# Bucketed attention with a gated product: 305 unread TensorE products put into the first batch's instruction order, and the score banks made fixed tiles

## The chip, the cores and the metric

One NeuronCore of one Trainium2 chip runs the whole program. The metric is device time in microseconds (us), the median of three runs. Inside the core, TensorE multiplies matrices (in the profile PE; its weight loads PEld), VectorE (DVE), ScalarE (ACT) and GpSimd (POOL) do elementwise work, and SyncE (SP) issues DMAs. The engines run on their own and wait for each other by semaphores; each engine executes its instructions in the order in which the program lists them. TensorE writes only to PSUM, which DVE and ACT read.

## The reference

Attention over 4 batches, 8 heads, 768 positions, 64 features; a key counts for a query only if both fall in the same of 64 buckets (signs of 6 projections). Its output, 3072 tokens by 512, then goes through a gated product.

```
q_bits = (einsum('bhsd,dk->bhsk', q, proj) > 0); k_bits likewise; bucket = sum of bits * 2**n
scores = where(q_bucket == k_bucket, q @ k.T / sqrt(64), -1e9)
attn = exp(scores - max); attn = attn / (sum(attn) + 1e-9); x = attn @ v   -> 3072 x 512
out = ((x @ w_a) * (x @ w_b)) @ w_out        (w_a, w_b: 512 x 1536; w_out: 1536 x 512)
```

## The kernel before

**Work.** Keys and queries are split into two half-precision parts and turned so that the features lie on partitions (`split`, with `kt`, `qt` the parts, `trk`, `trq` the turned copies, `hp` a ring of buffers for the second part with the bucket bits). The masking penalty is part of the same product as the scores. For each 128 queries of a head, `qtile` (L1194) makes one score tile `s` of 128 x 768 by four matmuls (L1207); DVE takes its maximum `mx` (L1227); DVE or POOL makes `sc` and `bias` (L1235, L1239); ACT takes the exponential `e` (L1248); `e` is turned, by TensorE through PSUM tiles `et` in the first eight tiles and by DMA later (`at`), and multiplied with `v` into `av` (L1261, L1276). A finished chunk goes into `xT` and through the gated product (`moe`: `ab` L1434 and L1442, `g` L1471, `o` L1507). In the first batch the weights are loaded in 36 DMAs (L926) through three staging places, rebuilt by ACT (L937, L947), POOL (L939) and DVE (L955) into `wz`, and bounded by TensorE products `gram_w`, `gram_wo` (L973) that DVE reduces to `wst`, `wost` (L661).

**PSUM.** A partition has eight banks of 512 fp32 columns. Tag `s` has two buffers of [128, 2, 512], two banks each; tag `ab` three of one bank, `av` one. A score tile uses columns 0 to 383 of each of the two banks of its buffer (`HALF` is 384). The turned keys and queries go through `s` buffers too: twelve 128x128 half-precision blocks fill columns 0 to 511 of the first bank and 0 to 255 of the second. Other small products take only the first bank, or an `ab` buffer.

**Order.** The kernel is first written down as a list of 3727 operations with costs (`Plan.op`), numbered as they are defined (`o.seq`). `Plan.issue` (L400) then plays them through by the keys in `PLACES` and by the free buffers, and calls each operation's function at L465; the order of these calls is the order on each engine. A buffer of `Buf` is given out when the first operation that uses it is played and comes free with the last. Semaphores between engines are put in by the framework: an instruction waits for earlier instructions of other engines that read or wrote what it touches.

Of the kernel before, what the change touches and what calls it, by code (L numbers as in the profile page):

```python
# [12 lines left out]
F32 = mybir.dt.float32  # L13
# [8 lines left out]
P = 128  # L22
# [3 lines left out]
HALF = S // 2  # L26
# [5 lines left out]
CH = 256  # L32
# [222 lines left out]
)  # L255
ENGINES = {
    17: "DVE", 20: "ACT", 27: "ACT", 33: "DVE", 36: "DVE", 43: "ACT", 49: "DVE", 52: "DVE", 53: "ACT DVE",
    59: "DVE", 69: "POOL", 81: "ACT", 84: "ACT", 85: "POOL", 91: "ACT", 106: "ACT", 108: "ACT", 117: "POOL",
# [82 lines left out]
class Buf:  # L341


    def __init__(self, plan, pool, tag, bufs, shape, dtype, name, share=None, ring=None):
        self.ring = ring
        self.plan, self.pool, self.tag, self.bufs = plan, pool, tag, bufs
        self.limits = [((pool, tag), bufs)]
        if share:
            self.limits.append(((pool, tag, share[0]), share[1]))
        self.shape, self.dtype, self.name = shape, dtype, name  # L350
        self.real, self.left, self.free_at = None, 0, 0.0
# [15 lines left out]
class Plan:  # L367
# [3 lines left out]

    def __init__(self):
        self.ops, self.writer, self.readers = [], {}, {}

    def op(self, eng, dur, fn, key, r=(), w=(), svc=0.0, hold=(), sbuf=False):
        o = Op()
        o.eng, o.dur, o.fn, o.key, o.svc, o.sbuf = eng, dur, fn, key, svc, sbuf
        o.seq = len(self.ops)
        preds = set()
        for x in r:  # L380
            if x in self.writer:
                preds.add(self.writer[x])
            self.readers.setdefault(x, []).append(o.seq)
        for x in w:
            if x in self.writer:
                preds.add(self.writer[x])
            preds.update(self.readers.pop(x, ()))
            self.writer[x] = o.seq
        preds.discard(o.seq)
        o.preds = preds  # L390
        o.bufs = []
        for x in (*r, *w, *hold):
            x = x[0] if isinstance(x, tuple) else x
            if isinstance(x, Buf) and x not in o.bufs:
                o.bufs.append(x)
                x.left += 1
        self.ops.append(o)
        return o

    def issue(self):  # L400
        ops = self.ops
        for o, place in zip(ops, PLACES):
            o.key = place
            o.eng = ENGINES.get(o.seq, o.eng)
        for o in ops:
            o.succs, o.npred, o.ready = [], len(o.preds), 0.0
        for o in ops:
            for p in o.preds:
                ops[p].succs.append(o)
        free = {e: 0.0 for e in ("PE", "ACT", "DVE", "POOL", "SP")}  # L410
        ready = {e: [] for e in free}
        for o in ops:
            if not o.npred:
                for e in o.eng.split():
                    ready[e].append(o)
        live = {}
        dma_free = 0.0
        held = set()
        port = 0.0
        done = 0  # L420
        now = 0.0
        events = [0.0]
        releases = []

        def can(o):
            need = {}
            for b in o.bufs:
                if b not in held:
                    for k, _ in b.limits:
                        need[k] = need.get(k, 0) + 1  # L430
            return all(live.get(k, 0) + need.get(k, 0) <= n for b in o.bufs for k, n in b.limits)

        while done < len(ops):
            now = heapq.heappop(events)
            while events and events[0] <= now:
                heapq.heappop(events)
            while releases and releases[0][0] <= now:
                _, k = heapq.heappop(releases)[0:2]
                for x in self.tags[k]:
                    live[x] -= 1  # L440
            for e in free:
                if free[e] > now:
                    continue
                if e == "POOL" and port > now:
                    continue
                best = None
                shut = e == "DVE" and free["POOL"] > now + PORT_WAIT
                for o in ready[e]:
                    if shut and o.sbuf:
                        continue  # L450
                    if o.ready <= now and (best is None or (o.key, o.seq) < (best.key, best.seq)) and can(o):
                        best = o
                if best is None:
                    continue
                o = best
                for x in o.eng.split():
                    ready[x].remove(o)
                for b in o.bufs:
                    if b not in held:
                        held.add(b)  # L460
                        for k, _ in b.limits:
                            live[k] = live.get(k, 0) + 1
                dur = o.dur
                if isinstance(dur, dict):
                    o.fn(e)  # L465
                    dur = dur[e]
                else:
                    o.fn()
                end = now + dur
                if e == "DVE" and o.sbuf:  # L470
                    end = max(now, free["POOL"]) + dur
                    port = end
                free[e] = end
                if o.svc:
                    dma_free = max(dma_free, end) + o.svc
                    fin = dma_free + DMA_TAIL
                else:
                    fin = end + (PE_TAIL if e == "PE" else 0.0)
                for b in o.bufs:
                    b.left -= 1  # L480
                    b.free_at = max(b.free_at, fin + HOP)
                    if not b.left:
                        if b.ring is not None:
                            b.ring.append(b.real)
                        if not hasattr(self, "tags"):
                            self.tags = []
                        self.tags.append([k for k, _ in b.limits])
                        heapq.heappush(releases, (b.free_at, len(self.tags) - 1))
                        heapq.heappush(events, b.free_at)
                for s in o.succs:  # L490
                    s.ready = max(s.ready, end if s.eng == e and not o.svc else fin + HOP)
                    s.npred -= 1
                    if not s.npred:
                        for x in s.eng.split():
                            ready[x].append(s)
                        heapq.heappush(events, max(now, s.ready))
                heapq.heappush(events, end)
                done += 1
            if not events and done < len(ops):
                raise RuntimeError("no operation can start")  # L500
        return now
# [3 lines left out]
def attention_moe(ctx: ExitStack, tc: tile.TileContext, q, k, v, proj, w_a, w_b, w_out, cst, out):  # L505
    nc = tc.nc
# [3 lines left out]
    pp = ctx.enter_context(tc.tile_pool(name="pp", bufs=1, space=PSUM))  # L510

    plan = Plan()
    op = plan.op

    def buf(tag, shape, dtype, name, bufs=2, pool=None, share=None):
        return Buf(plan, pool or p2, tag, bufs, shape, dtype, name, share)

    def f3(name, share):


        return buf("f3", [P, S], F32, name, NF3, share=share)

    def two(name, share):


        return buf("two", [P, 2 * S], F16, name, NTWO, share=share)

    def psum(name, tag="s"):

        return buf(tag, [P, 2, CH if tag == "ab" else 512], F32, name, {"s": 2, "ab": 3}[tag], pp)  # L530

    def f32(ap):
        return ap.bitcast(F32)
# [51 lines left out]
    onesr = cp.tile([P, P], BF16, tag="onesr", name="onesr")  # L585
# [79 lines left out]
    def gram(x, cols, key, toks, stat, stok, tag, name):  # L665


        ps = psum(f"gram_{name}", tag)

        def products():  # L670
            high = x().bitcast(BF16).rearrange("p (n two) -> p n two", two=2)[:, :, 1]
            for i in range(cols // P):
                c = high[:, i * P : (i + 1) * P]
                nc.tensor.matmul(ps.t[:, 0, :P], lhsT=c, rhs=c, start=i == 0, stop=i == cols // P - 1)

        op("PE", 0.11 * cols / P, products, key, r=toks, w=[ps])
        op("DVE", 0.3, lambda: most_of(ps, stat), key, r=[ps], w=[stok])
# [861 lines left out]
    for b in range(NB):  # L1539
        chunks = [m for m in range(NCHUNK) if CHUNKS[m][0] == b]  # L1540
        sus = [(m, half) for m in chunks for half in range(CHUNKS[m][2])]
        for i, (m, half) in enumerate(sus):
            start, nt = done, CHUNKS[m][2]
            h0, nh = heads(m, half)
            tag = "ab" if start < 2 * UT else "s"
# [65 lines left out]
```

## Time and profile before

| what | us |
|---|---|
| median of 3 runs (902.34 to 904.34) | 903.89 |
| the profiled execution | 904.85 |
| its span, first to last instruction | 903.1 |
| outside the span | 1.75 |
| TensorE busy, share of the span | 874.0, 97% |
| VectorE busy | 625.5, 69% |
| ScalarE busy | 572.5, 63% |
| mean granted TensorE clock | 0.986 |

A busy share of 97% is an average over a first stage, in which all engines prepare keys, queries and weights, and a long second one. The clock is given as a share of full speed; its two levels are 1.2 GHz (0.5) and 2.4 GHz (1.0).

### The profile page before, as it was taken

The numbers are of one execution on the slowest core, as the hardware profiler recorded it, in microseconds if no ns is written. First come the engines' busy times: TensorE is split into PE (matmuls) and PEld (weight loads), VectorE is DVE, ScalarE is ACT, GpSimd is POOL, SyncE is SP. The second block draws the span as 40 slices with busy tenths as digits, with TensorE's granted clock in tenths as the row PEclk, the third lists the DMA queues.
The fourth block names the chain that finished last, engine by engine and source line by source line (L and its number), as shares of the span: only waits on it lengthen the run. The fifth ranks groups of instructions, "written<-read, shape, count | busy, mean of one in ns | idle before, by whom it ended". The sixth has DMA issues, their size and how long they took to land.

```text
span 903.1 us, 24309 instructions
## 1 busy us (share of the span) xinstructions
PE 874.0 (97%) x9761; PEld 676.1 (75%) x9761; DVE 625.5 (69%) x1446; ACT 572.5 (63%) x1124; POOL 451.5 (50%) x377
## 2 busy tenths in 40 slices
PE   5798999999999999999999999999999999999998
PEld 4587787777877777777777777777777777777775
DVE  6899878897778666677776686777778676633211
ACT  5985656777767777666666665667676566654222
POOL 1255456455736665644445556545556457544111
PEclk9798999999999999999999999999999999999999
DMA  8997766589998999997986798799996757754100
GB/s 309 282 328 192 129 124 147 133 187 209 183 232 155 160 157 171 181 215 157 181 169 124 142 188 163 123 205 165 184 187 140 129 133 133 147 95 96 35 24 24
DMA packets 430433, 145.31 MB, mean 161 GB/s; under 512 B 404080, under 2 KB 422640, under 8 KB 430320
## 3 DMA queue, kind: packets, MB, share of 16 engines
q1 hardware_dynamic: 430320, 143.77, 77.4%
q8 instruction: 76, 1.25, 0.6%
q14 instruction: 37, 0.30, 0.1%
HBM read 37.82 MB, written 6.29 MB: 49 GB/s over the span
## 4 chain that ended last, share of the span: by engine, by line
PE 84%; DVE 7%; DMA 3%; issue 3%; ACT 2%; POOL 1%; SPq 0%; DVEq 0%; POOLq 0%; ACTq 0%
PE ab L1442 36%; PE o L1507 19%; PE s L1207 13%; PE av L1276 10%; PE ab L1434 4%; DMA wz<-in_moe_w_out_dram 1%; DVE mx L1227 1%; DVE wz L955 1%; DMA rq<-in_q_dram 1%; DVE wz L898 1%; DMA v<-in_v_dram 1%; DMA at<-a 1%; PE qb L780 0%; PE av L1261 0%; ACT wz L937 0%
## 5 line engine op out<-in xcount | busy, mean ns | idle before, releaser
L641 POOL TENSOR_TENSOR a<-e,a 128x768 f16<-128x768 f32 x184 | 310.5, 1692 | 202.1 <-DVE a L638 87.5
L1442 PE MATMUL ab<-xT,wz 128*128 128x256 f16 (+1 forms) x3456 | 377.5, 264 | 1.5 <-DVE g L1471 1.1
L1442 PEld LDWEIGHTS <-wz 128*128 128x128 f16 x3456 | 310.9, 98 | 52.4 <-issue 3.6
L1248 ACT ACTIVATE e<-s,bias,sc 128x768 f32<-128x768 f32 x192 | 189.6, 988 | 109.5 <-DVE bias L1239 87.5
L1227 DVE TENSOR_REDUCE mx<-s 128x1 f32<-128x768 f32 x192 | 182.6, 953 | 64.9 <-PE s L1207 59.8
L1507 PE MATMUL o<-wz,g 128*128 128x512 f16 (+1 forms) x840 | 215.7, 392 | 0.1
L1487 POOL TENSOR_TENSOR g<-g,g 128x256 f16<-128x256 f32 x132 | 96.4, 730 | 169.5 <-ACT g L1482 157.0
L1207 PE MATMUL s<-trk,trq 76*128 76x384 f16 (+1 forms) x768 | 158.3, 331 | 3.3 <-ACT e L1248 2.4
L1471 DVE SCALAR_TENSOR_TENSOR g<-ab,ab,a 128x256 f32<-128x256 f32 x132 | 63.3, 479 | 106.5 <-ACT a L1463 89.2
L1276 PEld LDWEIGHTS <-at 128*128 128x128 f16 x3312 | 116.9, 98 | 16.8 <-DMA at<-a 1.8
L1507 PEld LDWEIGHTS <-g 128*128 128x128 f16 x792 | 73.9, 98 | 68.8
L1276 PE MATMUL av<-vh,at 128*128 128x64 f16 x2208 | 121.6, 193 | 1.4 <-DMA at<-a 1.4
L1463 ACT ACTIVATE a<-ab,ab 128x256 f32<-128x256 f32 x132 | 62.1, 471 | 95.2 <-PE ab L1442 79.3
L1207 PEld LDWEIGHTS <-trq 76*128 76x128 f16 (+1 forms) x768 | 70.7, 99 | 45.0 <-issue 8.8
L638 ACT CAST a<-e 128x768 f16<-128x768 f32 x105 | 87.0, 829 | 3.9 <-DMA at<-a 1.9
L1482 ACT CAST g<-g 128x256 f16<-128x256 f32 x132 | 53.0, 401 | 51.2 <-DVE g L1471 40.9
L1276 PE MATMUL av<-vl,at 128*128 128x64 f16 x1104 | 62.4, 193 | 0.0
L638 DVE CAST a<-e 128x768 f16<-128x768 f32 x71 | 42.2, 596 | 14.0 <-ACT e L1248 13.2
L1434 PE MATMUL ab<-xT,wz 128*128 128x128 f32 x384 | 48.0, 278 | 3.0 <-DVE wst L661 2.2
L1434 PEld LDWEIGHTS ab<-xT,wz 128*128 128x128 f32 x384 | 45.6, 192 | 5.4 <-DVE wst L661 2.4
L1239 DVE TENSOR_SCALAR bias<-mx,sc 128x1 f32<-128x1 f32 x180 | 38.5, 214 | 6.3
L1235 DVE TENSOR_SCALAR sc<-mx,cq 128x1 f32<-128x1 f32 x180 | 38.1, 212 | 4.8
(169 smaller groups left out, 778.5 us busy)
## 6 DMA issues: line engine op xcount, KB each, us to landing
rk<-in_k_dram SPq DMA_DIRECT2D x16, 384.0 KB, 4.1
rq<-in_q_dram SPq DMA_DIRECT2D x24, 256.0 KB, 3.4
wz<-in_moe_w_a_dram SPq DMA_DIRECT2D x12, 512.0 KB, 5.1
wz<-in_moe_w_b_dram SPq DMA_DIRECT2D x12, 512.0 KB, 5.4
wz<-in_moe_w_out_dram SPq DMA_DIRECT2D x12, 512.0 KB, 4.7
out_dram<-osb SPq DMA_DIRECT2D x24, 256.0 KB, 2.5
vr<-in_v_dram SPq DMA_DIRECT2D x12, 384.0 KB, 4.6
at<-a SPq DMA_TRANSPOSE x184, 3.5
```

The source lines that it names most:

```text
L638: {"ACT": nc.scalar.copy, "DVE": nc.vector.tensor_copy, "POOL": nc.gpsimd.tensor_copy}[e](out=out, in_=x)
L641: (nc.gpsimd if e == "POOL" else nc.vector).tensor_tensor(out=out, in0=x, in1=y, op=ALU.subtract)
L1207: nc.tensor.matmul(ps.t[:, jj, :HALF], lhsT=trq.t[rows, i, (2 * j + h) * nt + t], rhs=tr.t[rows, i, k0 : k0 + NT // 2].rearrange("p n s -> ...
L1227: lambda: nc.vector.tensor_reduce(out=mx.t[:, col], in_=halves(ps.t), axis=AX.XY, op=ALU.max, negate=True),
L1248: lambda: nc.scalar.activation(flat2(e.t), halves(ps.t), AF.Exp, bias=bias.t[:, col], scale=sc.t[:, col], accum_out=sm.t[:, u : u + 1],),
L1276: nc.tensor.matmul(av.t[:, u, :], lhsT=at.t[:, a + kt, :], rhs=w.t[:, h, kt, :], start=i == 0, stop=i == 3 * NT - 1,)
L1434: nc.tensor.matmul(pl.t[:, m, to], lhsT=wt32(m, cc, f), rhs=xt.t[:, cc * nt // NC, cc * nt % NC : cc * nt % NC + nt, :], start=cc == 0, st ...
L1442: nc.tensor.matmul(pl.t[:, m, to], lhsT=wt(m, wi, cc, f), rhs=xt.t[:, cc * nt // NC, xi, cc * nt % NC : cc * nt % NC + nt, :], start=i == ...
L1463: lambda a=a, pl=pl, gr=gr, sc_of=sc_of: nc.scalar.activation(a.t, pl.t[:, 0, :CH], AF.Copy, scale=sc_of(gr)),
L1471: lambda a=a, g32=g32, pl=pl, gr=gr, sc_of=sc_of: nc.vector.scalar_tensor_tensor(out=g32.t, in0=pl.t[:, 1, :CH], scalar=sc_of(gr + 1), in1 ...
L1487: lambda g=g, g32=g32, g_of=g_of: nc.gpsimd.tensor_tensor(out=g_of(g[1]), in0=g32.t, in1=g_of(g[0]), op=ALU.subtract),
L1507: nc.tensor.matmul(po[u].t.rearrange("p a b -> p (a b)"), lhsT=x()[:, us], rhs=w, start=f == 0 and i == 0, stop=f == NF - 1 and i == len(t ...
```

## The change

A product of the 128x128 tile of ones `onesr` with itself, written to a place that nobody reads, is issued in the numbers of `FILLS` just before the operation with that number. The place is columns 384 to 511 of the second bank of the first `s` buffer. The two `s` buffers are no longer given out by the pool: they are fixed tiles, handed round by the ring that `Buf` already has.

```diff
+FILLS = {
+    7: 30, 13: 4, 77: 3, 15: 1, 79: 2, 29: 3, 99: 12, 86: 15, 47: 9, 196: 12, 42: 11, 51: 11, 67: 11, 119: 4, 58: 6,
+    308: 16, 74: 10, 152: 19, 181: 6, 320: 9, 171: 6, 132: 6, 159: 5, 218: 8, 545: 13, 170: 4, 269: 12, 402: 16,
+    386: 5, 420: 28, 592: 8,
+}
...
         self.ops, self.writer, self.readers = [], {}, {}
+        self.fill = None
...
                 dur = o.dur
+                if o.seq in FILLS:
+                    self.fill(FILLS[o.seq])
                 if isinstance(dur, dict):
                     o.fn(e)
...
+    banks = [pp.tile([P, 2, 512], F32, tag=f"s{i}", name=f"s{i}") for i in range(2)]
+    idle_at = banks[0][:, 1, HALF:]
+
+    def fill(n):
+
+        for _ in range(n):
+            nc.tensor.matmul(idle_at, lhsT=onesr, rhs=onesr, start=True, stop=True)
+
+    plan.fill = fill
...
-        return buf(tag, [P, 2, CH if tag == "ab" else 512], F32, name, {"s": 2, "ab": 3}[tag], pp)
+        if tag == "s":
+            return Buf(plan, pp, tag, 2, [P, 2, 512], F32, name, None, banks)
+        return buf(tag, [P, 2, CH], F32, name, 3, pp)
```

The keys stand in the order in which the plan plays them. The list below says, for the groups from the twelfth on, which operation follows, when it started before, and which reader of the second bank of the first `s` buffer the plan plays last ahead of the group. Ahead of the first eleven groups (102 products) that reader had ended in the trace before TensorE came to the group.

| key | products | operation that follows, and its start before | last reader ahead of it |
|---|---|---|---|
| 51 | 11 | `kt` transposes, 25.38 | DVE `mx` at 24.55 |
| 67, 119, 58 | 11, 4, 6 | `kt` 29.98, `et` 31.11, `kt` 32.46 | ACT `e` at 28.86 (67, 119), ACT `trk` at 30.99 (58) |
| 308, 74, 152 | 16, 10, 19 | `ps_w` 36.98, `kt` 37.93, score 40.28 | DVE `trk` at 36.84 |
| 181 | 6 | score 42.44 | ACT `trk` at 40.13 |
| 320, 171, 132 | 9, 6, 6 | `gram_wo` 44.59, score 46.90, `av` 48.81 | DVE `mx` at 43.97 |
| 159 | 5 | `et` 50.25 | ACT `e` at 49.43 |
| 218 | 8 | score 59.53, in the other `s` buffer | DVE `mx` at 59.59 |
| 545, 170 | 13, 4 | `gram_q` 67.03, `av` 67.97 | ACT `e` at 65.90 |
| 269 | 12 | score 72.94, in the other `s` buffer | DVE `mx` at 73.58 |
| 402 | 16 | first `ab` 77.56 | DVE `mx` at 73.58 |
| 386, 420 | 5, 28 | `gram_w` 83.48, `ab` 90.58 | ACT `e` at 77.77 |
| 592 | 8 | score 113.49 | ACT `e` at 105.24 |

## Rows read from the trace of the kernel before

**Rows 1.** Busy time by stretch: stretch, length, PE, PEld, DVE, ACT, POOL, clock, DMA.
```profile
0.00:90.58 90.58, 69.70 (x692) 60.05 (x692) 77.56 (x163) 65.10 (x92) 33.01 (x37) 0.87 0.87 277
90.58:226.00 135.42, 132.74 (x1628) 105.93 (x1629) 112.62 (x243) 90.61 (x168) 72.02 (x57) 1.00 0.78 155
226.00:500.00 274.00, 273.59 (x3204) 209.60 (x3203) 195.98 (x489) 192.80 (x397) 151.77 (x123) 1.00 0.92 174
```

**Rows 2.** Waits of DVE, 0 to 90.58: total us, times, longest.
```profile
DVE wz L955 <- ACT wz L937: 1.5, 1, 1.5
DVE mx L1227 <- PE s L1207: 1.1, 2, 0.8
DVE mx L1227 <- PE ps_k L612: 1.1, 1, 1.1
...
DVE po_t_k L624 <- PE ps_k L612: 0.7, 1, 0.7
DVE wst L661 <- PE gram_w L973: 0.5, 2, 0.3
...
DVE vst L661 <- PE gram_v L674: 0.3, 1, 0.3
```

**Rows 3.** Busy time by stretch around the low clock, columns as in rows 1.
```profile
21.00:29.00 8.00, 6.37 (x51) 5.36 (x52) 6.42 (x16) 8.00 (x10) 3.29 (x4) 0.57 0.80 268
38.00:50.00 12.00, 9.82 (x67) 7.38 (x67) 9.43 (x14) 10.57 (x16) 4.95 (x8) 0.57 0.93 253
69.00:77.00 8.00, 7.78 (x48) 6.53 (x47) 7.63 (x13) 5.54 (x7) 4.71 (x4) 0.57 1.09 252
```

**Rows 4.** Timeline of PE: start, us, instruction, [idle before, releaser].
```profile
26.61 1.91 PE L973 MATMUL gram_w<-wz 128*128 128x128 bf16 x16
...
37.93 0.83 PE L759 MATMUL kt<-identh,hp 128*128 128x128 f16 x12 [0.79 <-DVE trk L638]
40.28 1.44 PE L1207 MATMUL s<-trk,trq 76*128 76x384 f16 x4 [1.52 <-ACT e L1248]
...
59.53 0.81 PE L1207 MATMUL s<-trk,trq 76*128 76x384 f16 x4 [0.56 <-ACT e L1248]
...
72.94 1.49 PE L1207 MATMUL s<-trk,trq 76*128 76x384 f16 x4
...
90.58 1.16 PE L1434 MATMUL ab<-xT,wz 128*128 128x128 f32 x8 [2.25 <-DVE wst L661]
...
97.22 0.82 PE L1207 MATMUL s<-trk,trq 76*128 76x384 f16 x4
...
106.64 1.08 PE L973 MATMUL gram_wo<-wz 128*128 128x128 bf16 x16
107.56 1.93 PE L1507 MATMUL o<-wz,g 128*128 128x512 f32 x4
```

**Rows 5.** Timeline of DVE, columns as in rows 4.
```profile
36.84 0.94 DVE L638 COPY trk<-kt 128x1536 f16<-128x1536 f16 x1
...
41.76 0.96 DVE L1227 TENSOR_REDUCE mx<-s 128x1 f32<-128x768 f32 x1
...
48.42 0.96 DVE L1227 TENSOR_REDUCE mx<-s 128x1 f32<-128x768 f32 x1 [0.81 <-PE s L1207]
...
59.59 0.95 DVE L1227 TENSOR_REDUCE mx<-s 128x1 f32<-128x768 f32 x1
...
60.95 0.95 DVE L1227 TENSOR_REDUCE mx<-s 128x1 f32<-128x768 f32 x1
...
73.58 0.95 DVE L1227 TENSOR_REDUCE mx<-s 128x1 f32<-128x768 f32 x1
...
75.04 0.95 DVE L1227 TENSOR_REDUCE mx<-s 128x1 f32<-128x768 f32 x1
...
98.08 0.96 DVE L1227 TENSOR_REDUCE mx<-s 128x1 f32<-128x768 f32 x1 [0.53 <-PE s L1207]
```

**Rows 6.** The chain that ended last: start, us, what.
```profile
31.36 5.68 DMA wz<-in_moe_w_out_dram
```

## The prediction

> **What bounds the kernel now.** I read the page first, then the busy time by stretches, then the waits of TensorE and DVE in the first stretch, and last the timelines of both engines side by side around each group of products. The stretches divide the span in two. From 90.58 us on TensorE has hardly a gap: 132.74 of 135.42 us busy, then 273.59 of 274.00 [rows 1]. Whatever moves the moment at which it enters this stretch moves the end by nearly as much. Before 90.58 us TensorE is busy 69.70 of 90.58 us and so idle for 20.9 us, and DVE is busy 77.56 us [rows 1]. What opens the long stretch is a DVE result: TensorE waits 2.25 us for `wst` [rows 4]. So the price of this change is read from DVE before 90 us: what takes waits out of DVE's order there is a gain, what puts waits in is a loss, and idle time of TensorE alone is worth nothing.
>
> **What the low clock costs.** In three stretches, 21 to 29, 38 to 50 and 69 to 77 us, the mean granted clock is 0.57 [rows 3]: 28 us with 0.43 missing, 12.0 us of clock. The same sixteen 128x128 products take 1.91 us there and 1.08 us later [rows 4], four score matmuls 1.49 against 0.82 us [rows 4]. But DVE waits for TensorE in all these 90 us only 1.1 + 1.1 + 0.7 + 0.5 + 0.3 = 3.7 us [rows 2] (the first wait of all, for the projection, hangs on a load and is left out). 3.7 us is therefore the most that a clock held up can bring, unless another engine behind DVE gains too.
>
> **How much of the 3.7 us comes through.** 2.4 us (1.1 + 0.7 + 0.3, and half of the 0.5, rounded up) lie before 30 us. Behind them DVE stands still for 1.5 us until ACT has rebuilt a weight [rows 2], and ahead of that the chain passes through a weight load that took 5.68 us from 31.36 us on [rows 6]. An earlier DVE meets the same load, so this part counts only as far as the load is issued earlier. It is issued when ACT has freed its staging place, and ACT is busy all 8.00 of the 8 us from 21 to 29 [rows 3], so only an earlier start of ACT's work comes through. Bounds: 0 and 2.4 us; I take 0.4, near the lower end, because the DMA engines are 0.80 to 0.93 busy there [rows 3] and an earlier issue mostly queues longer. The 1.1 us belong to two score tiles, the second at 48.42 us [rows 5]. What the products do there (next part) costs 0.3 us, and DVE is held again by rebuilt weights before 60; bounds 0 and 0.8, I take 0. The last 0.2, before 77 us, is netted below. Kept: 0.4 us.
>
> **The products themselves.** One costs 57.5 ns at full clock: sixteen such take 107.56 - 106.64 = 0.92 us from start to start [rows 4]. At the low clock 1.91/16 = 119 ns bounds it. All 305 make 17.5 us, which the 20.9 us of TensorE's idle time could hold. What decides is whether a group can run inside the wait that it stands in. A group writes to a bank of the first `s` buffer, other columns than those in use. I take it that the framework orders it by the bank, so that a group waits until the last reader that the plan played ahead of it has finished. No row before shows a product into free columns of a bank that is being read, so the cost is bounded: nothing if only the columns count, and the reader's end minus the operation's old start, plus the products, if the bank counts. I take the second. The Trainium skill, page "PSUM — Partial Sum Buffer", section "PSUM bank collisions raise a hardware error", says that accesses of two engines have to be kept apart by bank and quadrant, not by address; by that rule the second bound holds, and it speaks against this change.
>
> By groups, with the table of the change:
> - The first eleven groups find no open reader and run in the waits. They cost nothing: the cover is TensorE's own idle time, and where a group is longer than its wait (15 products, 0.86 us) what comes late is bucket bits, for which DVE has other work queued.
> - 67 and 58 stand before operations that wait for the very reader; 17 products, 1.0 us, come on top of that wait. `trk` on ACT comes later by about half a microsecond, hidden by the load for which ACT and then DVE wait.
> - 308, 74 and 152 may start when DVE's copy ends at 36.84 + 0.94 = 37.78 us [rows 5]. Then 16 products, a `kt` turn of some 0.7 us and 10 and 19 products follow: 37.78 + 0.92 + 0.1 + 0.58 + 0.7 + 1.09 = 41.2 us instead of 40.28 [rows 4] for the score tile, and its maximum, 0.86 us after the score's start (97.22 to 98.08 [rows 4, 5]), at 42.05 instead of 41.76 [rows 5]: 0.3 us, counted above. If the clock stays up, the score tiles behind it are 0.67 us shorter each, which covers 181, 320, 171 and 132.
> - 159 waits some 0.2 us for an exponential; DVE has more than that queued.
> - 218: the score started at 59.53 us, released by ACT [rows 4]. Now the eight products wait for the `mx` that ends at 59.59 + 0.95 = 60.54 [rows 5]; 8 x 57.5 = 0.46 us, so the score starts at 61.0 and its maximum at 61.0 + 0.86 = 61.9 instead of 60.95 [rows 5]. Behind that maximum DVE's order is full until 90 us, and nothing else can pass it: **0.95 us lost**.
> - 545 and 170: 17 products, 1.0 us, on top of the wait; DVE is then 0.95 us late itself, which covers it.
> - 269: the score started at 72.94 [rows 4]. Its twelve products wait for the `mx` that ends at 73.58 + 0.95 = 74.53 [rows 5]; 0.69 us and 0.86 us later is 76.1 instead of 75.04 [rows 5], 1.1 us. The wait of 0.2 us for `gram_w` behind it goes: **0.9 us lost**.
> - 402, 386, 420 and 592 find no open reader, or no longer; the 28 products of 420 take 1.6 of the 2.25 us [rows 4].
>
> The fixed tiles change nothing by themselves: two buffers, handed round as they come free, as before.
>
> **Sum.** -0.4 + 0.95 + 0.9 = +1.45 us. The profiled execution took 904.85 us, of which 903.1 are span; with the sum, 906.3. The median of the runs is 0.96 us below the profiled execution, so I predict **905.3 us**. About 0.2%, 1.8 us, is what a measurement of this kernel can tell from no change, so the likeliest case lies just inside it.
>
> **Rivals.**
> A, the forecast: bank order holds, the clock stays up. 903.4 to 907.2 us (kept gain 1.5 to 0, losses 1.0 to 3.3). Chance 0.42.
> B, the clock falls all the same. With 269 TensorE would stand for up to 2.5 us before the twelve products, longer than the gaps of before. If it falls there, the products take 12 x 61 ns = 0.74 us more, the score tile 0.67 and the sixteen `gram_w` products 0.83 [rows 4]: 2.2 us on top, 907.5, up to 909. For it: the longest wait is not filled but made. Against: before 90.58 us TensorE stood for 2.25 us [rows 4] and the stretch after it has clock 1.00 [rows 1]. Chance 0.17.
> C, faster: the groups 218 and 269 are not held, because only columns count. Then nothing is lost at DVE and 1 to 3.7 us of DVE's waits [rows 2] come through: 900.2 to 902.9, most likely 901.9. It decides from the point where the score at 59.53 starts no later than before relative to the DVE work around it. Chance 0.23.
> D, the whole clock loss comes back: 12.0 us of clock [rows 3] would give 891.9. Against it DVE waits for TensorE 3.7 us only [rows 2]. The Trainium skill, page "TensorE: Matmul & The Clock Gate", section "Terms", prices throttled time in this way, as the time times the share of pulses missing; the rows here agree with it for TensorE's own instructions, not for the time. Chance 0.03.
> E, no effect: DVE makes the 1.9 us good, as its work before 90 us is stretched wherever POOL runs beside it, and a shift may undo that. 903.2 to 904.6. Chance 0.15.
>
> **Numbers.** Faster by over 0.2% (below 902.1): C 0.20, D 0.03, A 0.01, together 0.24. Slower (above 905.7): B 0.17, A 0.16, E 0.01, together 0.34. Same: 0.42. The range takes in A, E, most of B and the nearer part of C: 901.0 to 908.8, leaving out D, some 0.08 of C and a little of B. As it holds cases of both signs, the forecast's own range is the 903.4 to 907.2 of A.
>
> **What the profile after would show.** Right: clock 1.00 from some 10 us on, except perhaps around 73 to 77; `mx` of the eighth and ninth score tiles, adjacent before (59.59 and 60.95), some 1.9 us apart, DVE waiting for TensorE between them; the same before the `mx` that followed at 75.04; the products of 218 and 269 released by DVE; entry into the long stretch at 91.5 to 92.5 us. Wrong: products of 218 and 269 that start while an `mx` of the first buffer still runs (C); a clock of 0.5 around 75 us (B); entry before 90 us (C), or the weight loads of the first 40 us landing 2 us earlier.

## The result, and the profile after

The changed kernel takes 913.48 us, the median of 4 runs (912.02 to 919.28), beside 903.37 us for the kernel before (902.34 to 904.34): a ratio of 1.0124, 95% interval [1.0078, 1.0171]. Ratios are taken over all the runs and not from the two medians, whose quotient is 1.0112 here; differences in us are differences of medians. The forecast was 905.3 us, its range 901.0 to 908.8. The profiled execution is the longest of the four, 919.28 us with a span of 917.4; the spans of the others are 910.1 to 912.4 at a mean clock of 0.994, here it is 0.988. So its rows exaggerate the loss by some 6 us, and the shares of the loss are read from the experiments, not from this one trace. Line numbers are 20 higher than before in most places. The name `s` now stands for everything that is written to the two fixed tiles, so `kt`, `qt` and some of the small products appear under it too.

Busy time by stretch, columns as in [rows 1]; the first two answer to those rows, the next three to [rows 3]:
```profile
0.00:103.85 103.85, 84.56 (x990) 76.60 (x990) 80.64 (x167) 66.63 (x94) 31.33 (x38) 0.90 0.79 245
103.85:240.00 136.15, 133.15 (x1639) 106.24 (x1637) 110.45 (x239) 89.92 (x167) 71.77 (x55) 1.00 0.81 152
21.00:29.00 8.00, 6.25 (x74) 5.71 (x74) 4.62 (x11) 6.28 (x7) 2.49 (x3) 0.79 0.67 223
38.00:50.00 12.00, 9.49 (x134) 8.25 (x133) 9.64 (x17) 8.67 (x12) 5.22 (x7) 1.00 1.02 269
69.00:77.00 8.00, 8.00 (x46) 7.34 (x46) 5.58 (x10) 5.20 (x9) 2.64 (x4) 0.50 0.56 177
```
The first stretch is 13.27 us longer (103.85 against 90.58 us), the rest of the span 1.0 us. TensorE has 990 matmuls in it in place of 692 and is busy 14.9 us more; its idle time of 20.9 us, which should have taken them in, only fell to 19.3. The clock is better from 21 to 50 us and worse from 69 to 77.

Waits of TensorE, 0 to 130 us (total, times, longest); L529 is the new product:
```profile
PE s L529 <- DVE mx L1247: 5.8, 4, 1.9
PE s L529 <- DVE st_q L681: 3.0, 2, 2.4
PE s L529 <- ACT trq L658: 2.3, 1, 2.3
PE av L1281 <- ACT at L658: 1.7, 1, 1.7
...
PE s L529 <- ACT trk L658: 1.2, 2, 0.9
PE s L529 <- DVE trk L658: 1.1, 1, 1.1
```
Waits of DVE, 0 to 103.85 us, to be read beside [rows 2]:
```profile
DVE mx L1247 <- PE s L1227: 4.4, 5, 2.2
...
DVE mx L1247 <- PE ps_k L632: 3.3, 1, 3.3
...
DVE at L658 <- PE et L1203: 2.1, 2, 1.1
DVE st_q L681 <- PE s L529: 1.3, 1, 1.3
DVE wost L681 <- PE gram_wo L993: 1.0, 1, 1.0
```
The products wait for readers, and DVE waits for what stands behind the products: 12.1 us in these five rows, where it waited 3.7 us for TensorE before (the first wait of all, 4.1 us in both, is left out again).

The products in the timeline of TensorE, with the score or `ab` behind them, beside [rows 4]:
```profile
21.66 0.83 PE L529 MATMUL s<-onesr 128*128 128x128 bf16 x12 [2.34 <-ACT trq L658]
...
65.66 0.61 PE L529 MATMUL s<-onesr 128*128 128x128 bf16 x8 [1.93 <-DVE mx L1247]
66.11 0.87 PE L1227 MATMUL s<-trk,trq 76*128 76x384 f16 x4
...
83.75 1.42 PE L529 MATMUL s<-onesr 128*128 128x128 bf16 x12 [1.62 <-DVE mx L1247]
84.96 1.48 PE L1227 MATMUL s<-trk,trq 76*128 76x384 f16 x4
...
102.29 1.72 PE L529 MATMUL s<-onesr 128*128 128x128 bf16 x28 [2.45 <-DVE st_q L681]
103.85 1.11 PE L1454 MATMUL ab<-xT,wz 128*128 128x128 f32 x8
```
DVE, beside [rows 5], and the one ACT row that the first group waits for:
```profile
26.39 0.96 DVE L1247 TENSOR_REDUCE mx<-s 128x1 f32<-128x768 f32 x1 [3.31 <-PE ps_k L632]
...
64.66 0.95 DVE L1247 TENSOR_REDUCE mx<-s 128x1 f32<-128x768 f32 x1
67.08 0.96 DVE L1247 TENSOR_REDUCE mx<-s 128x1 f32<-128x768 f32 x1 [0.97 <-PE s L1227]
...
82.75 0.95 DVE L1247 TENSOR_REDUCE mx<-s 128x1 f32<-128x768 f32 x1
86.48 0.96 DVE L1247 TENSOR_REDUCE mx<-s 128x1 f32<-128x768 f32 x1 [2.19 <-PE s L1227]
...
101.76 0.28 DVE L681 TENSOR_REDUCE wst<-gram_w 128x1 bf16<-128x128 f32 x1
101.96 0.28 DVE L681 TENSOR_REDUCE st_q<-s 128x1 bf16<-128x128 f32 x1
```
```profile
20.60 1.01 ACT L658 COPY trq<-s 128x1024 f16<-128x1024 f16 x1
```
Two readers in these rows never touch the bank into which the products go. The copy `trq` reads 1024 half-precision columns, the 512 fp32 columns of the first bank; it ends at 21.61, and the twelve products into the second bank start at 21.66. `st_q` reads 128 columns of the first bank, ends at 102.24, and the 28 products start at 102.29.

### The profile page after: what moved, and what is told of

It is laid out like the page before. It is cut to its first block, busy times and chain, and to the rows that moved or that the text cites. A ratio compares the mean times of both kernels' runs of the same rounds, so it can differ in the third digit from the quotient of the medians.

```text
span 917.4 us, 24955 instructions
## 1 busy us (share of the span) xinstructions
PE 889.3 (97%) x10066; PEld 692.9 (76%) x10066; DVE 629.0 (69%) x1446; ACT 573.2 (62%) x1124; POOL 448.0 (49%) x377
## 4 chain that ended last, share of the span: by engine, by line
PE 84%; DVE 7%; issue 3%; DMA 3%; ACT 2%; SPq 1%; POOL 1%; DVEq 0%; ACTq 0%; POOLq 0%
PE ab L1462 32%; PE o L1527 19%; PE s L1227 12%; PE av L1296 9%; PE ab L1454 4%; PE s L1462 3%; DVE mx L1247 1%; DMA wz<-in_moe_w_a_dram 1%; DVE wz L975 1%; PE s L529 1%; PE s L800 1%; PE av L1281 1%; DMA wz<-in_moe_w_out_dram 1%; DVE wz L918 1%; DMA at<-a 1%
## 5 line engine op out<-in xcount | busy, mean ns | idle before, releaser
L1462 PE MATMUL ab<-xT,wz 128*128 128x256 f16 (+1 forms) x3168 | 344.4, 263 | 1.7 <-DVE g L1491 1.3
L1483 ACT ACTIVATE a<-ab,ab 128x256 f32<-128x256 f32 x120 | 56.5, 471 | 74.8 <-PE ab L1462 59.1
L1491 DVE SCALAR_TENSOR_TENSOR g<-ab,ab,a 128x256 f32<-128x256 f32 x120 | 57.5, 479 | 66.0 <-ACT a L1483 59.9
```

The lines of the kernel that those rows point to most:

```text
L1462: nc.tensor.matmul(pl.t[:, m, to], lhsT=wt(m, wi, cc, f), rhs=xt.t[:, cc * nt // NC, xi, cc * nt % NC : cc * nt % NC + nt, :], start=i == ...
L1483: lambda a=a, pl=pl, gr=gr, sc_of=sc_of: nc.scalar.activation(a.t, pl.t[:, 0, :CH], AF.Copy, scale=sc_of(gr)),
L1491: lambda a=a, g32=g32, pl=pl, gr=gr, sc_of=sc_of: nc.vector.scalar_tensor_tensor(out=g32.t, in0=pl.t[:, 1, :CH], scalar=sc_of(gr + 1), in1 ...
```

## The experiments

Each profile is split in three: the **entry**, the start of the `ab` of 420 (90.58 us before); the **second gate**, the `av` product near 221 us that waits for a turned tile `at`; and the tail behind it. The table gives each against the profile of before, beside the medians, which are of several runs each. The last two columns are the wait at the second gate itself (1.43 us before) and the mean granted clock in the 10 us from the gate on (1.00 before).

| run | products | median minus before's, us | entry | entry to second gate | tail | wait at the gate | clock behind it |
|---|---|---|---|---|---|---|---|
| whole change | 305 | +10.1 | +13.27 | +0.76 | +0.27 | 1.60 | 1.00 |
| tiles alone | 0 | -0.3 | -2.23 | -0.91 | +2.34 | 0.62 | 0.83 |
| one for each group | 31 | +5.9 | +2.24 | +0.81 | +2.25 | 1.94 | 0.84 |
| first nine groups | 79 | +1.8 | -1.45 | +1.17 | +1.58 | 1.80 | 0.83 |
| held groups left out | 157 | +1.9 | -1.43 | +0.84 | +2.09 | 1.81 | 0.83 |
| 196 alone | 12 | +2.1 | -0.35 | +0.70 | +0.55 | 0.66 | 1.00 |
| 218 and 269 | 20 | +7.8 | +3.56 | +3.13 | +0.31 | 2.45 | 1.00 |
| 420 alone | 28 | +6.2 | +1.25 | +1.55 | +3.40 | 3.08 | 0.69 |
| free buffer only | 190 | +3.9 | -1.72 | +1.75 | +2.77 | 2.56 | 0.83 |
| 218 and 269, second buffer | 20 | +2.4 | -3.28 | +2.04 | +3.54 | 2.77 | 0.69 |
| 420, one product | 1 | +0.1 | -1.77 | -0.97 | +0.74 | 0.56 | 1.00 |
| without 218, 269, 420 | 257 | +2.1 | -0.36 | +0.55 | +0.61 | 0.72 | 1.00 |
| all, eight groups moved | 305 | +4.2 | +2.07 | +1.24 | +0.79 | 1.87 | 1.00 |

Two kernels that measure like before, the tiles alone and the single product, enter 2.23 and 1.77 us earlier in their profiles. So an entry of one profile says nothing below some 2 us.

The tails go with the last column. Where the clock is 1.00 behind the gate, the tail is 0.27 to 0.79 us longer than before; at 0.83 and 0.84, which is 1.6 to 1.7 us of clock, 1.58 to 2.77; at 0.69, 3.1 us of clock, 3.40 and 3.54. Here TensorE has hardly a gap [rows 1], and lost clock comes out as time. The length of the wait alone does not sort the clock: it is 0.83 behind a wait of 0.62 us, and 1.00 behind one of 2.45.

**Tiles alone.**
```diff
-    7: 30, 13: 4, 77: 3, 15: 1, 79: 2, 29: 3, 99: 12, 86: 15, 47: 9, 196: 12, 42: 11, 51: 11, 67: 11, 119: 4, 58: 6,
...
+FILLS = {}
```


> The two fixed tiles without any product (FILLS empty). Theory H (a group of products is held until every reader of the first score buffer that was issued ahead of it has ended, also readers of its other bank, and TensorE stands in order behind it): 902.5 to 904.3 us, as before, low clock in the same three stretches. Rival W (the products' own time on TensorE) and rival K (the clock falls at worse places): the same, 903.4. Rival P (the fixed tiles make semaphores stricter than the pool did): 906 us or more.

904.24 us against 904.55, 0.9992 [0.9975, 1.0009]. The fixed tiles cost nothing; the products make the whole loss. The low clock lies in the first two of the three stretches as before (0.57 each); the third has 0.97, and 77 to 95 us has 0.92.

**One product for each group.**
```diff
+FILLS = {7: 1, 13: 1, 77: 1, 15: 1, 79: 1, 29: 1, 99: 1, 86: 1, 47: 1, 196: 1, 42: 1, 51: 1, 67: 1, 119: 1, 58: 1, 308: 1, 74: 1, 152: 1, 181: 1, 320: 1, 171: 1, 132: 1, 159: 1, 218: 1, 545: 1, 170: 1, 269: 1, 402: 1, 386: 1, 420: 1, 592: 1}
```


> Each of the 31 groups cut to one product, 31 instead of 305. H: the waits stay and only the products' own time behind a held wait goes (1.6 us in the group of 28, 0.4 at 218, 0.6 at 269, some 1.3 around 196 and 42): 907 to 911 us, and TensorE still waits more than 2 us at 196 and at 420. W: a tenth of the loss is left, 904 to 905 us. K: hardly any work keeps the clock up, so it falls in at least the three stretches of before; 904 to 912, without the waits at 196 and 420.

910.4 us, 1.0072 [1.0049, 1.0095]: a tenth of the products, more than half of the loss. TensorE, timeline, the single products of 196, 218 and 269:
```profile
22.24 0.22 PE L525 MATMUL s<-onesr 128*128 128x128 bf16 x1 [2.34 <-ACT trq L654]
...
62.77 0.22 PE L525 MATMUL s<-onesr 128*128 128x128 bf16 x1 [1.51 <-DVE mx L1243]
...
77.35 0.22 PE L525 MATMUL s<-onesr 128*128 128x128 bf16 x1 [3.38 <-DVE mx L1243]
77.40 1.44 PE L1223 MATMUL s<-trk,trq 76*128 76x384 f16 x4
```
They are held 2.34, 1.51 and 3.38 us (2.34, 1.93 and 1.62 with all the products), and behind the longest the score tile runs at the low clock (1.44 us against 0.82 at full [rows 4]). At 420 the one product waits only 0.20 us, where more than 2 us were expected. More than half of the cost is the place in the order, not the work.

**First nine groups, and held groups left out.** The first keeps the groups up to 47. The second leaves out thirteen groups: those that wait for a reader in the profile after, and neighbours of theirs.
```diff
+FILLS = {7: 30, 13: 4, 77: 3, 15: 1, 79: 2, 29: 3, 99: 12, 86: 15, 47: 9}
```
```diff
+FILLS = {7: 30, 13: 4, 77: 3, 15: 1, 79: 2, 29: 3, 99: 12, 86: 15, 47: 9, 119: 4, 74: 10, 152: 19, 171: 6, 132: 6, 170: 4, 402: 16, 386: 5, 592: 8}
```


> Only the first nine groups (79 products, up to key 47), none of which waits for a reader of the buffer in the profile after. H: nothing is lost; the first 15 us run at full clock and DVE is some 0.3 us earlier at 20 us: 902.4 to 903.8 us. W: 79 of 305 products, a quarter of the loss: 905 to 906 us. K: the clock falls from 21 us as before: 903 to 904.

> 157 of the 305 products stay; left out are the thirteen groups that stood for a reader of the buffer in the profile after or stand directly behind one that did (196, 42, 51, 67, 58, 308, 181, 320, 159, 218, 545, 269, 420). H: 902.0 to 904.5 us. W: half of the loss, 907 to 909 us. K: with half of the products gone the clock falls again in two or three stretches; 903 to 908.

906.39 us, 1.0024 [1.0006, 1.0042], and 906.42 us, 1.0023 [1.0003, 1.0043], against 904.55. Both lie above the ranges of H, and the loss is the same with 79 products as with 157. The second, by stretch, beside [rows 3], and behind the second gate:
```profile
21.00:29.00 8.00, 4.97 (x69) 3.81 (x68) 7.59 (x19) 8.00 (x10) 3.39 (x4) 1.00 0.83 279
38.00:50.00 12.00, 8.73 (x106) 7.08 (x106) 10.96 (x18) 10.14 (x15) 5.13 (x7) 1.00 0.88 264
69.00:77.00 8.00, 5.34 (x55) 4.41 (x54) 7.66 (x14) 5.77 (x7) 4.56 (x4) 1.00 1.09 251
220.00:230.00 10.00, 9.14 (x112) 7.05 (x113) 6.03 (x13) 6.45 (x12) 6.95 (x6) 0.83 0.92 213
```
Here the products do all that can be hoped of them: clock 1.00 in the three stretches that had 0.57, which lacked 12.0 us of clock. The entry is no earlier than with the tiles alone (89.15 and 88.35 us), and the time is not shorter. DVE's waits for TensorE up to there, the first left out, hardly fell: 3.1 us, beside 3.9 with the tiles alone. So the clock ahead of the entry is worth nothing that can be measured, net of what the products themselves cost. Why these two kernels are 1.8 us slower stays open: their profiles show a longer wait at the second gate and a low clock behind it (10 us at 0.83, 1.7 us), but the profile of the tiles alone shows that clock too (0.84 at 220 to 230).

**196 alone.**
```diff
+FILLS = {196: 12}
```


> Only the twelve products before the operation 196 (gram_q at 20.60). The last reader of the first score buffer ahead of them is ACT's copy of turned queries, which reads the first bank alone. H by the whole buffer: the products start only when that copy ends, about 22 us, TensorE standing for 2 us or more before them; gram_q comes 1.5 us late or more, the first score maximum after 25.7 instead of 24.55 us, and part of it is hidden behind the weight load at 37 us: 904.5 to 906.5 us. H by the bank (what the prediction said): the products run from 19.6 us on in the wait, 902.8 to 904.6 us. W: twelve products, no measurable change.

905.39 us against 903.26, 1.0027 [1.001, 1.0045]. The same hold of 2.34 us. The maximum that started at 48.42 before starts at 49.90, the one at 73.58 at 75.08 [rows 5]: 1.5 us late. In four profiles without a hold there (tiles alone, one product of 420, first nine groups, held groups left out) the two start at 47.51 to 48.83 and 72.29 to 74.06, so the hold is still in DVE's order at 75 us. By its time alone this kernel can't be told from those that lose 1.8 us without any hold.

**218 and 269 alone, and in the second buffer.**
```diff
+FILLS = {218: 8, 269: 12}
```
```diff
+SECOND = (218, 269)
...
-    idle_at = banks[0][:, 1, HALF:]
+    idle_at = [x[:, 1, HALF:] for x in banks]
...
-            nc.tensor.matmul(idle_at, lhsT=onesr, rhs=onesr, start=True, stop=True)
+            nc.tensor.matmul(idle_at[second], lhsT=onesr, rhs=onesr, start=True, stop=True)
```


> Only the 8 + 12 products before the score tiles 218 and 269. H: both groups start when a running score maximum of the first buffer ends; the maxima of the eighth and ninth tiles, back to back before, stand 1.9 us or more apart; DVE loses 0.95 and 0.9 us as predicted, or more where the clock is low: 905.3 to 907.5 us. W: 20 of 305 products, 0.7 us at most.

> The groups of 218 and 269 alone (20 products), as in the run before this that had them in the first s buffer and came out at 911.1 us, but written to the same columns of the second s buffer, which the score behind each group is about to fill and which nobody is reading then. Hold by the whole buffer: TensorE no longer waits for a maximum ahead of these products (5.0 us in two waits before), and what stays is their own work, 20 products at about 0.055 us, 1.1 us in all; the ab of 420 starts within 1.2 us of 90.6 us, and the time is 903 to 905.5 us. Work and place in the order: the buffer does not matter, the time stays at 909 to 912 us.

First buffer: 911.1 us against 903.26, 1.0085 [1.0061, 1.0109]. Second buffer: 906.11 against 903.72, 1.0027 [1.0008, 1.0047]. TensorE's two groups, first in the one, then in the other:
```profile
62.82 0.91 PE L525 MATMUL s<-onesr 128*128 128x128 bf16 x8 [1.87 <-DVE mx L1243]
63.53 1.49 PE L1223 MATMUL s<-trk,trq 76*128 76x384 f16 x4
...
78.80 0.83 PE L525 MATMUL s<-onesr 128*128 128x128 bf16 x12 [3.10 <-DVE mx L1243]
```
```profile
59.84 0.61 PE L526 MATMUL s<-onesr 128*128 128x128 bf16 x8 [0.32 <-ACT e L1265]
60.28 0.82 PE L1224 MATMUL s<-trk,trq 76*128 76x384 f16 x4
...
71.67 0.83 PE L526 MATMUL s<-onesr 128*128 128x128 bf16 x12
```
Same products, same place in the order, another buffer: the holds of 1.87 and 3.10 us are gone, and with them 5.4 of 7.8 us. The first buffer's 911.1 us lie above what was expected (905.3 to 907.5), the second's 906.11 lie 0.6 us above. The 2.4 us that are left with the second buffer are not settled: the products' own work is an estimated 1.1 us, but the entry in this profile is the earliest of all, and what is long is the gate's wait and the tail. In the first buffer DVE's two pairs of maxima stand 3.30 and 2.66 us apart (61.82 and 65.12, 77.80 and 80.46) where they were 1.36 and 1.46 [rows 5]: 1.94 and 1.20 us. The low clock behind the first hold (the score at 1.49 us; 0.95 behind the second) makes the first larger.

**420: 28 products, one product.**
```diff
+FILLS = {420: 28}
```
```diff
+FILLS = {420: 1}
```


> Only the 28 products before the operation 420 (ab at 90.58), which stands in a wait of 2.25 us. The last reader ahead is DVE's reduction st_q, which reads 128 columns of the first bank. H by the whole buffer: the products start when st_q ends, 0.2 us after the wst that releases ab, and take 1.6 us: ab is 1.8 us late against wst, 905.0 to 906.8 us. H by the bank (the prediction): they fill the wait, 902.8 to 904.6 us.

> One product ahead of 420 in place of 28 (the 28 alone came out at 909.5 us). Work behind the hold: the 28 products can only start when st_q has been read, some 0.2 us behind wst, so their 1.6 us lay on the path; with one product the ab of 420 starts at most 0.3 us late, and the time is 903 to 905.5 us. The hold itself is the cost: the one product waits as long as the 28 did, and the time stays at 908 to 910 us.

28 products: 909.5 us against 903.26, 1.0069 [1.0046, 1.0091], above the expected 905.0 to 906.8. One: 903.86 against 903.72, 1.0002 [0.9984, 1.002]. TensorE with 28, and at the second gate:
```profile
90.27 1.72 PE L525 MATMUL s<-onesr 128*128 128x128 bf16 x28 [1.07 <-DVE st_q L677]
91.83 1.11 PE L1450 MATMUL ab<-xT,wz 128*128 128x128 f32 x8
...
224.25 0.50 PE L1292 MATMUL av<-vh,at 128*128 128x64 f16 x6 [3.08 <-DMA at<-a]
```
```profile
220.00:230.00 10.00, 6.61 (x61) 4.51 (x59) 5.38 (x13) 7.01 (x15) 6.10 (x6) 0.68 1.15 200
```
The products start when `st_q` has been read, 0.2 us behind the `wst` for which the `ab` waits, so all 1.56 us of them come on top. That explains 1.3 to 1.8 of the 6.2 us. The rest of this profile arises at the second gate: `ab` 1.25 us late, the gate 2.80 us late, the wait there 3.08 us where it was 1.43, and then the clock at 0.68 for 10 us, 3.2 us of clock. The chain that ended last, of this run and of before, ahead of the gate:
```profile
216.32 1.68 POOL a L657 x2
218.00 6.20 DMA at<-a
```
```profile
216.85 4.55 DMA at<-a
```
The turned tile starts 1.15 us late and takes 1.65 us longer to land. With one product `st_q` had ended at 87.71 us, before TensorE came to the product at 88.75, so in that profile it was not held at all. All four runs of the 28 products (908.03 to 911.11) lie above all fifteen of the kernel before beside them (up to 906.8), so it is no single bad execution. Why the landing takes longer stays open.

**Free buffer only.** 190 products: the groups that were to find one of the two buffers without a reader, seven of them in the second.
```diff
+FILLS = {7: 30, 13: 4, 77: 3, 15: 1, 79: 2, 29: 3, 99: 12, 86: 15, 47: 9, 196: 12, 42: 11, 67: 11, 58: 6, 308: 16, 74: 10, 170: 4, 269: 12, 402: 16, 386: 5, 592: 8}
+SECOND = (196, 42, 67, 58, 308, 74, 269)
```


> 190 products: the groups 7 to 47, 170, 402, 386 and 592 into the first score buffer, and 196, 42, 67, 58, 308, 74 and 269 into the second one, which has no open reader there; the groups 51, 119, 152, 181, 320, 171, 132, 159, 218, 545 and 420 left out. H: no group stands for a reader by more than 1 us, the clock stays up in the first 40 us, and the long stretch is entered between 88 and 90.5 us: 901.5 to 904.5 us. W: 190 of 305 products, 909 us. K: the clock falls at 40 and 70 us as before: 903 to 905.

907.19 us against 903.26, 1.004 [1.0016, 1.0064]; 901.5 to 904.5 was expected. 3.9 us over the kernel before where the whole change is 10.1 us over it, with 62% of its products, but no better than the 157. The groups 269 and 196 are not held in the second buffer, but others are: 74 stands 1.99 us for an exponential that reads the second buffer and 308 stands 0.76 us for a maximum, and DVE waits 2.5 us once for a score. So this run is not free of holds, and it can't say what products cost without them. Its profile has the gate wait at 2.56 us and the clock at 0.91 from 220 to 240.

**Without 218, 269 and 420; and all 305, eight groups moved.**
```diff
+FILLS = {7: 30, 13: 4, 77: 3, 15: 1, 79: 2, 29: 3, 99: 12, 86: 15, 47: 9, 196: 12, 42: 11, 51: 11, 67: 11, 119: 4, 58: 6, 308: 16, 74: 10, 152: 19, 181: 6, 320: 9, 171: 6, 132: 6, 159: 5, 545: 13, 170: 4, 402: 16, 386: 5, 592: 8}
```
```diff
+SECOND = (196, 42, 67, 58, 308, 74, 218, 269)
```


> The whole change without the groups of 218, 269 and 420 (257 products). If these three carry most of the 10 us, what is left is the 906.4 us of the 157 products that find no reader, plus about 2 us for 196 and something for the other held groups: 907.5 to 910 us, and the ab of 420 starts 4 to 9 us earlier than in the whole change (103.85 us). If the cost lies in the many groups together, whichever they are: 911.5 to 914 us.

> All 305 products, with eight groups (196, 42, 67, 58, 308, 74, 218, 269) written to the second s buffer in place of the first. Hold by the whole buffer: the waits for a reader at 196, 218 and 269 go, those at 51, 181, 159 and 420 stay; 908 to 911 us, at least 2 us under the whole change. The number of products decides: 912 to 915 us, like the whole change.

905.79 us, 1.0023 [1.0002, 1.0044], and 907.95 us, 1.0052 [1.0031, 1.0073], both against 903.72. 48 of the 305 products carry 8.0 of 10.1 us. With every product kept and only eight groups in the other buffer, 5.9 of the 10.1 us are gone. The first came out 1.7 us under the lower end of its expectation: 257 products, held groups among them, cost no more than 196 did by itself. In the second a new hold appears, 2.60 us for an exponential ahead of 74, and DVE waits 4.5 us once; a group moved to the other buffer meets the other buffer's readers. No version beats the kernel before.

## Why the prediction was wrong

Two steps failed. The order by the bank put 196 and 420 at nothing, and the loss at 218 and 269 was mis-sized. These three, 218, 269 and 420, carry 8.0 of the 10.1 us. A third, that the end follows the entry, held only in part.

**What bounds the kernel** held in part. DVE's order decides what happens before 90 us, and DVE's new waits (12.1 us in the five rows shown) stand where the time goes. But "whatever moves the moment at which it enters this stretch moves the end by nearly as much" is only half true: near 221 us there is a second gate, fed by POOL and by DMA turns, with its own wait and in some profiles its own fall of the clock. In the 20 products of the second buffer the entry is 3.28 us early and the span 2.3 us longer. The gate was in the chain of the kernel before (the 4.55 us of `at<-a`), and the prediction did not read it.

**What the low clock costs** was right for the stretches that it priced. At most 3.7 us to gain, 0.4 kept: with the clock at 1.00 through those stretches nothing measurable came, and DVE still waited 3.1 us for TensorE. The prediction did not price a clock that falls in the long stretch; behind the second gate 1.6 to 3.1 us of clock went with tails 1.58 to 3.54 us longer. The Trainium skill, page "TensorE: Matmul & The Clock Gate", section "Terms", counts throttled time as time times the missing share of pulses; that fits TensorE's instructions here (a score of 1.44 to 1.49 us against 0.82) and roughly the tails behind the gate, but ahead of the entry not the kernel's time.

**The first step that failed** is "I take it that the framework orders it by the bank". The order is by the whole two-bank buffer: the products into the second bank wait for `trq` (2.34 us in the whole change, with one product and with 196 alone) and for `st_q`, which read the first bank alone (the products start at 21.66 and 102.29 us, 0.05 us behind the ends of those reads). The table of the change lists readers of the second bank only, so two groups were called free that are not. The Trainium skill, page "PSUM — Partial Sum Buffer", section "PSUM bank collisions raise a hardware error", asks for accesses to be kept apart by bank and quadrant; what is waited for here is wider than that rule.

Three things follow from it:
- "The first eleven groups find no open reader": 196 waits 2.34 us and costs 2.1 us by itself, as much as the 257 products without 218, 269 and 420 together (the sum had -0.4 for them). But products that are never held lost 1.8 us, so not all of the 2.1 need be the hold's. The trace of before has the reader, in ACT's timeline:
```profile
20.95 1.01 ACT L638 COPY trq<-qt 128x1024 f16<-128x1024 f16 x1
```
- "420 ... the 28 products take 1.6 of the 2.25 us": they cannot use that wait, since `st_q` ends after `wst`. In DVE's timeline of before it ends at 90.73:
```profile
90.45 0.28 DVE L661 TENSOR_REDUCE st_q<-gram_q 128x1 bf16<-128x128 f32 x1
```
  With 28 products at the 1.56 us measured and the 0.05 us from a reader's end to the product, the `ab` could start at 92.34: 1.76 us late. 6.2 us of time were measured; the rest lies at the second gate and behind it, and its cause stays open.
- Rival C, that only the columns count, falls too: the products of 218 and 269 start 0.05 us behind the end of an `mx` that reads columns 0 to 383 alone.

**The second, 218 and 269: right mechanism, wrong size.** The places, the releaser and DVE's wait behind them are as predicted. 0.95 + 0.9 us were put down; DVE loses 1.94 + 1.20 us there with these groups alone, 1.06 + 2.27 in the profile after, and the time is 7.8 us longer. Where the score behind a hold ran at 0.87 and 0.95 us, DVE lost 1.06 and 1.20, near the forecast; where it ran at the low clock, 1.48 and 1.49 us, DVE lost 2.27 and 1.94. The sum left that clock out. It is rival B's mechanism, priced at 2.2 us and given 0.17. In the profile after the clock falls behind three waits of TensorE, those of 1.71 us (for an ACT copy, at 51.90), 1.93 us (218) and 1.62 us (269); by stretch:
```profile
52.00:56.00 4.00, 4.00 (x26) 3.60 (x27) 2.91 (x5) 4.00 (x6) 0.00 (x0) 0.64 0.97 337
...
68.00:72.00 4.00, 4.00 (x20) 3.40 (x19) 3.36 (x7) 1.98 (x3) 3.64 (x4) 0.50 0.45 134
...
84.00:88.00 4.00, 4.00 (x35) 3.31 (x34) 1.43 (x3) 0.00 (x0) 0.35 (x2) 0.60 1.02 196
```
With the two groups alone DVE's losses make 3.1 of the 7.8 us; another 3.1 us come between the entry and the second gate, why is not shown.

**Rival E and the tiles.** The tiles change nothing, as said (0.9992). DVE did not make good what was lost: the 1.5 us of 196 are still there at 75 us.

**The sum.** By medians: 8.0 us for 218, 269 and 420 in the company of the others, 2.1 for the remaining 257. The parts alone (7.8 + 6.2) are more than they are together; in the profiles each alone has a loss at the second gate or behind it (3.13 and 0.31, 1.55 and 3.40 us) that the whole change does not have (0.76 and 0.27). Not settled: why that landing varies, and the 1.8 us of the kernels whose products are never held.

## What to carry to other kernels

A dummy product is not free in an idle engine's wait: it stands in the engine's order, and what it waits for is set by everything that reads the tile into which it writes, the part that it does not touch included, so list the readers of the tile, not of the columns. Where it must be put, write it to the tile that the next instruction will write anyway (5.4 of 7.8 us came back by that), and list that tile's readers too: one group that was moved met a new hold of 2.60 us. And before clock is bought, look whether the engine behind it waits at all: 12.0 us of clock were worth nothing in the first stretch, where DVE waited 3.7 us for TensorE, while 1.6 to 3.1 us of it behind the second gate, where TensorE has hardly a gap, went with 1.58 to 3.54 us of time.

## What the runs showed of the hardware

The same DVE instructions take different times in two executions of the same order. Timeline of DVE, before and with the tiles alone, a pair of weight rebuilds in each:
```profile
78.14 4.43 DVE L955 SCALAR_TENSOR_TENSOR wz<-wz 128x1024 int32<-128x1024 int32 x2
```
```profile
77.22 2.98 DVE L971 SCALAR_TENSOR_TENSOR wz<-wz 128x1024 int32<-128x1024 int32 x2
```
1.45 us in one pair, with equal medians. With the maximum ahead of it, which starts at 75.04 before and at 74.47 with the tiles alone, this makes 2.0 of the 2.23 us between the two entries; differences below that were therefore taken from medians. The pair goes with POOL's work beside it. Where no POOL instruction runs in it (one for each group, 218 and 269) it takes 2.35 us; in the other twelve profiles, all with one or two of them beside it, 2.98 us in nine, 3.80 and 3.81 in two (420 alone, whole change), and 4.43 before. Why it is not the same in all twelve is not shown.
